# The first half of z with its last product on half the rows of the array, in an adaLN attention and gMLP block

## The chip, the cores and the metric

The kernel runs on one core of one Trainium2 chip. The core's engines work side by side, each through its own list in order: TensorE (PE: matmuls; PEld, the loads of their weights), VectorE (DVE), ScalarE (ACT), GpSimd (POOL), and SyncE (SP), which here issues the DMAs. An instruction that waits holds up everything behind it in its engine's list. The metric is the device time of one execution in microseconds (us); lower is better.

## The reference

```python
h = layernorm(x) * (1 + ca) + sa            # x: 2048 x 448
x = x + ga * attention(h)                   # 16 heads of 28
h = layernorm(x) * (1 + cb) + sb
z = gelu(h @ w_in)                          # w_in: 448 x 1792
z1, z2 = z[:, :896], layernorm(z[:, 896:])
g = w_sp @ z2 + b_sp[:, None]               # w_sp: 2048 x 2048
x = x + gb * ((z1 * g) @ w_out)             # w_out: 896 x 448
```

The six modulation vectors sa to gb come from `silu(c) @ w_mod`. The change lies in `z1`, and in one place at the start of `w_sp @ z2`.

## The kernel before

All is float32, and accuracy is kept by splitting each matmul operand into a high part (rounded by a copy to fp32r, the type of the matmul operands) and a low part (what is left, a subtraction on VectorE), and adding three products: high by high, high by low, low by high. For the 448 rows of `h` and `w_in` this makes 11 matmuls (`STEPS`, line 29): nine for the three full chunks of 128 rows, and two for the last 64 rows. For those, operand 6 of the features holds the high part in rows 0 to 63 and the low part in rows 64 to 127, operand 6 of the weights holds the high part twice, so step (6,6) gives high by high and low by high in one. Step (6,7) gives high by low: operand 7 of the weights has the low part in rows 0 to 63 and zeros in rows 64 to 127, so half of the array's rows do nothing.

The stages in order: modulation, layer norm and q, k, v; attention, head by head; the output projection `wo` (`wo_mm`, line 828) with layer norm two; the first half of z (`z1_unit`, line 1197); the second half (`z2_mm`, `z2_halves`, lines 1431 to 1451); the mix `w_sp @ z2` (line 1533), which goes through sums of blocks, so that fewer products are needed; gate and output.

**The first half of z.** The features are in four row groups g of 512 rows, `h2T[g]`, and z1 has seven column blocks f of 128, so there are 28 units, unit n = 7 g + f, in the order of n. A unit is 11 matmuls of 128x512 into one PSUM bank, a gelu on ScalarE (line 1204) into one of four slots of a buffer (slot n % 4), and a store of that slot to DRAM. Seven banks go round. Beside the units runs a list written out by hand, `H2_AT` (line 1239): after unit n it places the steps that make the features of later row groups. For group g they are: statistics and norm (`h2_stats`, `h2_norm`, VectorE with a power on POOL), a transpose on VectorE (`h2_turn`), a store to DRAM (`h2_put`, four DMAs), a load back in the shape that is wanted (`h2_load`, five DMAs), and `h2_group` (line 1184) for each chunk c: two activations (the scaled features, then their high part) and a subtraction on VectorE (the low part). Group 1 has its load after unit 0, its chunks 0 and 2 after unit 3, 1 after unit 4, 3 after unit 5. Group 2 has statistics to store after units 0 to 3, the load after 5, its chunks 0, 2, 1, 3 after units 8 to 11. Group 3: statistics to store after 4 to 7, load after 9, chunks after 13 to 16. Where steps of two groups stand behind one unit, the earlier group's come first. Between them stand the loads of `w_in`'s second half and its parts, and seven times (units 10 to 25) the load, the parts (`wout_part`, line 1227) and the store of `w_out`.

**The second half of z** has 16 tiles of 128 rows in two halves. It computes in pairs: `z2_halves` gives the (6,7) products of two halves to the upper and the lower 64 rows of the array. For that, `twin` holds the high part of the last 64 features a second time, in rows 64 to 127; DMAs write it (`twin_load`, line 1426) at the stage's start, from `h2T`. A tile's gelu is followed by its statistics, and by its norm `z2_norm` (line 1467), for tile 14 and 15 in the last rounds of the loop.

**The mix** begins with `w_split` (line 1409): ScalarE copies the high part of a block of w_sp, VectorE subtracts the low part.

Of the kernel before, what the change touches and what calls it, by code (L numbers as in the profile page):

```python
# [8 lines left out]
F32 = mybir.dt.float32  # L9
F32R = mybir.dt.float32r  # L10
AF = mybir.ActivationFunctionType
# [88 lines left out]
def tile_adaln_mha_gmlp(ctx, tc, x, wqkv, wo, w_in, w_spT, b_sp, w_out, cT, w_mod0, w_mod, out):  # L100
# [34 lines left out]
    def hview(heap, off, a, b):  # L135
        return heap[:, off : off + a * b].rearrange("p (a b) -> p a b", b=b)
# [13 lines left out]
    def sub(eng, dst, a, hi):  # L150
        eng.tensor_tensor(out=dst, in0=a, in1=hi.bitcast(F32), op=ALU.subtract)  # L151
# [872 lines left out]
    heapA = fh.tile([128, 8 * 896], F32R, name="heapA")  # L1024
    heapB = fh.tile([128, 8 * 896], F32R, name="heapB")
    xl3 = fh.tile([128, 7, 512], F32, name="xl3", tag="heapC")
    w1 = hview(heapA, 0, 8, 896)
    h2T = [hview(heapB, g * 3584, 7, 512) for g in range(2)]

# [114 lines left out]

    w1_lo(0, pool)
    w1_lo(1, pool)
# [37 lines left out]
    def h2_group(g, cs):  # L1184
        for c in cs:
            f, hi = t3b.tile([128, 512], F32, name="hfull"), h2T[g][:, c if c < 3 else 6, :]
            src = h2T[g][:, 3 + c, :].bitcast(F32)
            act.activation(f, src, AF.Identity, scale=cols["cb"][:, c : c + 1], bias=cols["sb"][:, c : c + 1])
            act.activation(hi, f, AF.Copy)
# [7 lines left out]
    def z1_unit(g, f):  # L1197
        ps_t = bank("z1_ps")
        for j, (a, b) in enumerate(STEPS):
            pe.matmul(ps_t, w1[:, b, f * 128 : (f + 1) * 128], h2T[g][:, a, :], start=j == 0, stop=j == NST - 1)  # L1200
# [3 lines left out]
        act.activation(zt, ps_t, AF.Gelu_apprx_tanh)  # L1204
        sp.dma_start(z1_scr[f * 128 : (f + 1) * 128, g * 512 : (g + 1) * 512], zt)

    for t in range(8, 12):
        wo_tile(t)
# [18 lines left out]
    def wout_part(f):  # L1227
        raw = wouts[f][0]
        dve.tensor_tensor(out=raw, in0=raw, in1=bcs["gb"], op=ALU.mult)
        hi, lo = (wo3.tile([128, D], F32R, name=f"wout_{i}") for i in range(2))  # L1230
        act.activation(hi, raw, AF.Copy)
        sub(dve, lo, raw, hi)
        wouts[f] = hi, lo
# [4 lines left out]

    H2_AT = {}
    for g, at_g in (  # L1240
        (1, ((0, h2_load), (3, h2_group, (0, 2)), (4, h2_group, (1,)), (5, h2_group, (3,)))),
        (2, ((0, h2_stats), (1, h2_norm), (2, h2_turn), (3, h2_put), (5, h2_load))),
        (2, ((8, h2_group, (0,)), (9, h2_group, (2,)), (10, h2_group, (1,)), (11, h2_group, (3,)))),
        (3, ((4, h2_stats), (5, h2_norm), (6, h2_turn), (7, h2_put), (9, h2_load))),
        (3, ((13, h2_group, (0,)), (14, h2_group, (2,)), (15, h2_group, (1,)), (16, h2_group, (3,)))),
    ):
        for n, fn, *a in at_g:
            H2_AT.setdefault(n, []).append((fn, g, *a))
    for g in range(NG):
        for f in range(7):  # L1250
            z1_unit(g, f)
            for fn, *a in H2_AT.get(7 * g + f, ()):
                fn(*a)
            if (g, f) in ((0, 4), (0, 5)):
                win_load(f - 4, (t3, t3b)[f - 4])
            for fn, n in ((wout_load, 10), (wout_part, 12), (wout_store, 13)):
                if 0 <= 7 * g + f - n < 14 and (7 * g + f - n) % 2 == 0:
                    fn((7 * g + f - n) // 2)
            if g == 1 and f in (3, 5):
                win_prep(f // 4, dve)  # L1260
                win_load(2 + f // 4, (t3, t3b)[f // 4])
            if g == 2 and f in (3, 5):
                win_prep(2 + f // 4, dve)
# [48 lines left out]
    def wouts_load(g):  # L1312
        for at_g, i, f in WOUT_AT:
            if at_g == g:
                if (i, f) == (0, 0):
                    tbuf.append(wp.tile([128, 5120], F32R, name="wouts", tag="tw", bufs=1))
                if (i, f) == (1, 4):
                    tbuf.append(wp.tile([128, 1536], F32R, name="wouts2", tag="once", bufs=1))
# [15 lines left out]
    def z_sum(p):  # L1334
        if p >= NM:
            return
        for d, a, b, op in MIX[p][0]:
            if d == ONCE:
                once[:] = [wp.tile([128, 1536], F32, name="once", tag="once", bufs=1).rearrange("p (t c) -> p t c", c=384)]
# [81 lines left out]
    tz = ph4.enter_context(tc.tile_pool(name="tz", bufs=2))  # L1421
    z_mv, z_st = {}, {}

    twin = wp.tile([128, 3, 512], F32R, name="twin", tag="once", bufs=1)

    def twin_load(g):
        sp.dma_start(twin[64:128, g % 3, :].bitcast(F32), h2T[g][0:64, 6, :].bitcast(F32))

    z2_ps = {}

    def z2_mm(t, hf, steps, start, stop):
# [42 lines left out]
    banks.append(7)  # L1474
    banks.sort(key=lambda k: k > 2)
    for g in range(3):
        twin_load(g)
    for t in range(NT + 1):
        if t < NT:
            for hf in range(2):  # L1480
                z2_mm(t, hf, STEPS[:-1], t % 4 < 2, t % 4 > 1)
                if t % 4 > 1:
                    z2_act(t, hf)
            if t % 4 > 1:
                z2_stats(t)
        if t % 4 == 1 and t < NT:
            for k in range(4):
                z2_halves(t - 1 + k, k > 1)
            if t == 1:
                twin_load(3)  # L1490
            for k in range(2):
                for hf in range(2):
                    z2_act(t - 1 + k, hf)
                z2_stats(t - 1 + k)
                z2_norm(t - 1 + k)
        if t % 4 == 3 or t % 4 == 0 and t:
            z2_norm(t - 1)
        if t == 8:
            heapB2.append(fh.tile([128, 8 * 896], F32R, name="heapB2", tag="heapB"))
            tbuf.append(wp.tile([128, 5120], F32, name="tbuf", tag="tw", bufs=1))  # L1500
        if t == 9:
            z_sum(0)
        if t in (10, 12):
            z_hi(t // 2 - 5)
            z_lo(t // 2 - 5)
        if t in (11, 13, 14):
            z6_split((11, 13, 14).index(t))
        if 9 <= t < 13:
            b_load(bts(t - 9), t - 9)
        if 11 <= t < 15:  # L1510
            w_load(t - 11)
        if t in (13, 15):
            w_split((t - 13) // 2)
# [209 lines left out]
```

## Time and profile before

| | |
|---|---|
| median of 3 runs | 1366.68 us (1366.61 to 1367.72) |
| the profiled execution | 1368.8 us, of which 1367.0 us are the span of the trace |
| PE / PEld busy | 1360.5 / 967.4 us |
| VectorE / ScalarE / GpSimd busy | 1111.7 / 803.5 / 357.7 us |
| granted TensorE clock | 0.999 on average |
| first half of z (L1200) | 308 matmuls, 898.78 to 968.9 us of the span |
| second half of z (L1437, L1451) | to 1038.6 us, then the mix |

A line such as L1200 is that line of the kernel. In a timeline each row has the start, the duration, the engine, the line, the operation with out<-in, how many were merged, and in brackets how long the engine stood idle before it and what ended that. SPq is SyncE's list of DMAs: a row there is the issue, and the data land later.

### The profile page before, as it was taken

How to read it: one execution, taken by the hardware profiler on the slowest of the kernel's cores; microseconds unless marked ns; L12 is line 12 of the kernel's file. 1: busy time of each engine (PE TensorE's matmuls, PEld its weight loads, DVE VectorE, ACT ScalarE, POOL GpSimd, SP SyncE). 2: the span in 40 equal slices, each digit the busy share in tenths (PEclk: the TensorE clock that was granted, in tenths of full speed). 3: DMA queues.
4: the chain of work that ended last, by engine and by line, in shares of the span. 5: the costliest groups of instructions: out<-in, count | busy, mean ns of one | idle time of the engine just before them, and what ended most of it. 6: DMA issues, size and time to landing. Idle time of an engine off the chain costs nothing.

```text
span 1367.0 us, 20774 instructions
## 1 busy us (share of the span) xinstructions
PE 1360.5 (100%) x7050; PEld 967.4 (71%) x7050; DVE 1111.7 (81%) x1764; ACT 803.5 (59%) x1475; POOL 357.7 (26%) x370
## 2 busy tenths in 40 slices
PE   9999999999999999999999999999999999999998
PEld 8888655555556555655565555788888888888898
DVE  7888999999999999999999991673458778999752
ACT  6624666776677667766776679556325545555411
POOL 2134434244544355654641002210011000000000
PEclk9999999999999999999999999999999999999999
DMA  7465747776677668777874110578714665788553
GB/s 281 142 169 182 222 132 225 210 233 198 217 228 224 189 203 250 231 214 222 247 219 118 43 44 24 182 215 269 246 31 155 223 200 176 258 289 260 177 165 109
DMA packets 144598, 260.72 MB, mean 191 GB/s; under 512 B 22184, under 2 KB 43050, under 8 KB 141946
## 3 DMA queue, kind: packets, MB, share of 16 engines
q1 hardware_dynamic: 141774, 255.22, 60.3%
q10 hardware_dynamic: 2718, 4.19, 0.9%
q8 instruction: 55, 0.90, 0.3%
q14 instruction: 51, 0.42, 0.1%
HBM read 177.67 MB, written 76.34 MB: 186 GB/s over the span
## 4 chain that ended last, share of the span: by engine, by line
PE 97%; DVE 2%; DMA 0%; issue 0%; ACT 0%; POOL 0%; POOLq 0%; SPq 0%; DVEq 0%; ACTq 0%
PE st_ps L745 19%; PE mt L713 17%; PE o_ps L760 17%; PE pq L408 5%; PE z_ps L1200 5%; PE acc L1540 5%; PE acc L1541 5%; PE acc L1539 5%; PE z_ps L1437 3%; PE wo_ps L832 3%; PE pv L390 2%; PE y_ps L1612 2%; PE y_ps L1610 2%; PE y_ps L1611 2%; PE acc L1549 1%; PE acc L1547 1%
## 5 line engine op out<-in xcount | busy, mean ns | idle before, releaser
L718 DVE TENSOR_REDUCE pm<-mt 128x1 f32<-128x512 f32 x1024 | 626.1, 677 | 7.8 <-PE mt L713 7.8
L749 ACT ACTIVATE P<-st_ps 128x512 f32<-128x512 f32 x1024 | 512.1, 648 | 201.4 <-PE st_ps L745 197.7
L745 PE MATMUL st_ps<-qst,kst 128*128 128x512 f32 x1024 | 408.4, 408 | 0.0
L713 PE MATMUL mt<-kst,qst 128*128 128x512 f32 x1024 | 401.5, 392 | 0.0
L745 PEld LDWEIGHTS st_ps<-qst,kst 128*128 128x128 f32 x1024 | 191.3, 188 | 127.9 <-DVE pm L718 53.2
L760 PE MATMUL o_ps<-P,V 128*32 128x512 f32 x2048 | 240.0, 597 | 0.0
L713 PEld LDWEIGHTS mt<-kst,qst 128*128 128x128 f32 x1024 | 192.4, 188 | 35.6 <-ACT P L749 1.5
L870 POOL TENSOR_TENSOR ws_raw<-ws_raw 128x512 f32<-128x512 f32 x112 | 144.0, 1290 | 176.0 <-DMA ws_raw<-in_w_spT_dram 108.3
L1414 ACT ACTIVATE heapB<-raw_sp 128x512 fp32r<-128x512 f32 x156 | 97.1, 630 | 99.4 <-PE acc L1541 75.9
L760 PEld LDWEIGHTS o_ps<-P,V 128*32 128x32 f32 x2048 | 58.9, 109 | 127.3 <-issue 91.3
L1539 PE MATMUL acc<-heapB,heapA 128*128 128x512 f32 x312 | 121.4, 389 | 0.0
L1541 PE MATMUL acc<-heapB,heapA 128*128 128x512 f32 x312 | 121.4, 389 | 0.0
L766 DVE TENSOR_TENSOR osb<-osb,o_ps 128x512 f32<-128x512 f32 x82 | 56.4, 687 | 61.9 <-PE o_ps L760 60.1
L151 DVE TENSOR_TENSOR heapB<-raw_sp,heapB 128x512 fp32r<-128x512 f32 x112 | 74.7, 687 | 27.9 <-ACT heapB L1414 27.7
L1540 PE MATMUL acc<-heapB,heapA 128*128 128x512 f32 x222 | 86.5, 390 | 0.5 <-DVE heapB L151 0.5
L1539 PEld LDWEIGHTS acc<-heapB,heapA 128*128 128x128 f32 x312 | 58.6, 188 | 12.1
L1541 PEld LDWEIGHTS acc<-heapB,heapA 128*128 128x128 f32 x312 | 58.6, 188 | 12.1
L408 PE MATMUL pq<-heapD,heapD 128*128 128x512 f32 x196 | 61.8, 390 | 0.0
L151 POOL TENSOR_TENSOR ws_raw<-ws_raw 128x512 fp32r<-128x512 f32 x44 | 56.6, 1287 | 3.5
L1540 PEld LDWEIGHTS acc<-heapB,heapA 128*128 128x128 f32 x222 | 41.7, 188 | 9.6 <-DVE heapB L151 0.9
L786 POOL TENSOR_TENSOR osb<-osb,rb 128x512 f32<-128x512 f32 x15 | 19.3, 1284 | 109.6 <-DMA rb<-r_scr 97.4
L408 PEld LDWEIGHTS pq<-heapD,heapD 128*128 128x128 f32 x196 | 36.7, 188 | 7.4
(229 smaller groups left out, 1637.7 us busy)
## 6 DMA issues: line engine op xcount, KB each, us to landing
ws_raw<-in_w_spT_dram SPq DMA_DIRECT2D x136, 256.0 KB
ws_scr<-ws_raw SPq DMA_DIRECT2D x112, 256.0 KB
ws_raw<-ws_scr SPq DMA_DIRECT2D x88, 256.0 KB
raw_sp<-ws_scr SPq DMA_DIRECT2D x88, 256.0 KB
raw_sp<-in_w_spT_dram SPq DMA_DIRECT2D x68, 256.0 KB
wl_scr<-ws_raw SPq DMA_DIRECT2D x44, 256.0 KB
kst<-qk_scr SPq DMA_DIRECT2D x45, 224.0 KB
qst<-qk_scr SPq DMA_DIRECT2D x45, 224.0 KB
```

The lines of the kernel that those rows point to most:

```text
L151: eng.tensor_tensor(out=dst, in0=a, in1=hi.bitcast(F32), op=ALU.subtract)
L408: pe.matmul(pq, wqk[:, b, m * 128 : (m + 1) * 128], hT[g][:, a, :], start=j == 0, stop=j == NST - 1)
L713: pe.matmul(mt, qst[h % 3][:, t * 128 : (t + 1) * 128], kst[h % 3][:, kb * 512 : (kb + 1) * 512], start=True, stop=True)
L718: dve.tensor_reduce(out=pms[h][:, t, kb : kb + 1], in_=mt, axis=AX.X, op=ALU.max)
L745: pe.matmul(st, kst[h % 3][:, kt * 128 : (kt + 1) * 128], qst[h % 3][:, qb * 512 : (qb + 1) * 512], start=True, stop=True)
L749: act.activation(p, st, AF.Exp, scale=SCALE)
L760: pe.matmul(o[32 * qb : 32 * qb + 32, :], V[:, u % NT, h, :], ptiles.pop((u, qb)), start=u == a, stop=u == e - 1)
L870: pool.tensor_tensor(out=a, in0=a, in1=b, op=ALU.add if W_SUMS[v][2] > 0 else ALU.subtract)
L1414: act.activation(hi, raw[0], AF.Copy)
L1539: pe.matmul(o, zh[:, c], hi, start=p < 2 and kt == 0, stop=False, skip_group_check=p > 1)
L1540: pe.matmul(o, zh[:, c], lo, start=False, stop=False, skip_group_check=p > 1)
L1541: pe.matmul(o, zl[:, c], hi, start=False, stop=kt == 3, skip_group_check=p > 1)
```

## The change

The first half of z is computed in pairs too. Units 0 to 3 of a row group run ten steps without the last and leave their banks open. Then three pairs of 64-row products follow: (0,1) and (2,3) close these four, (4,5) opens the next two. Units 4 and 5 run ten steps and close. Unit 6 keeps all eleven. An eighth bank makes room. The gelus and the stores of units 0 to 3 are all issued after the steps of `H2_AT` that stand behind unit 3. Those of units 4 to 6 stay behind their own unit, ahead of its steps. For group 0 `twin` is written by a DMA at the stage's start, ahead of the load for group 1. For groups 1 to 3 ScalarE writes it, in a third activation of `h2_group` for chunk 3; the slot is g % 3, so group 0's copy is loaded again ahead of the second half. Operand 7 of the weights has the low part in both halves of its rows, and the zeros go. Group 1's chunks move one unit up (behind 2, 3, 4). The parts of `w_out` get one buffer for two. The norms of tiles 14 and 15 move from the end of the second half into the mix, behind `w_split` of its blocks 2 and 3.

```diff
+    twin = ... tw.tile([128, 3, 512], F32R, name="twin", tag="once")
...
-    pool.memset(w1[64:128, 7, :].bitcast(F32), 0.0)
...
-            sub(eng, w1[0:64, 7, :], wraw[0][0:64, 3, :], w1[0:64, 6, :])
+            sub(eng, w1[:, 7, :], wraw[0][:, 3, :], w1[:, 6, :])
...
             act.activation(hi, f, AF.Copy)
+            if c == 3:
+                act.activation(twin[64:128, g % 3, :], f[64:128], AF.Copy)
...
+    def z1_halves(g, fs, start):
+        for f, src, r in zip(fs, (h2T[g][:, 6, :], twin[:, g % 3, :]), (slice(0, 64), slice(64, 128))):
+            if start:
+                z1_ps[f] = bank("z1_ps")
+            pe.matmul(z1_ps[f], w1[r, 7, f * 128 : (f + 1) * 128], src[r, :], start=start, stop=not start)
...
+    def z1_unit(g, f):
+        if (g, f) == (0, 0):
+            twin_load(0)
+        z1_mm(g, f, STEPS if f == 6 else STEPS[:-1], f < 4 or f == 6, f > 3)
+        if f == 3:
+            for fs in ((0, 1), (2, 3), (4, 5)):
+                z1_halves(g, fs, fs[0] == 4)
+
+    def z1_acts(g, f):
+        for k in range(4) if f == 3 else (f,) if f > 3 else ():
+            z1_act(g, k)
...
+    banks.append(7)
...
-        hi, lo = (wo3.tile([128, D], F32R, name=f"wout_{i}") for i in range(2))
+        hi, lo = (wo3.tile([128, D], F32R, name=f"wout_{i}", bufs=1) for i in range(2))
...
-        (1, ((0, h2_load), (3, h2_group, (0, 2)), (4, h2_group, (1,)), (5, h2_group, (3,)))),
+        (1, ((0, h2_load), (2, h2_group, (0, 2)), (3, h2_group, (1,)), (4, h2_group, (3,)))),
...
             z1_unit(g, f)
+            if f > 3:
+                z1_acts(g, f)
             for fn, *a in H2_AT.get(7 * g + f, ()):
                 fn(*a)
+            if f == 3:
+                z1_acts(g, f)
...
-    for g in range(3):
-        twin_load(g)
+    twin_load(0)
...
-        if t % 4 == 3 or t % 4 == 0 and t:
+        if t < NT - 1 and (t % 4 == 3 or t % 4 == 0 and t):
             z2_norm(t - 1)
...
         w_split(g + 2)
+        if g < 2:
+            z2_norm(NT - 2 + g)
```

`z1_act(g, f)` is the gelu into slot (7 g + f) % 4 and the store, as before.

More of the change, by code (lines that the diff above doesn't have):

```diff
@@ L1026, in tile_adaln_mha_gmlp, with twin_load @@
     xl3 = fh.tile([128, 7, 512], F32, name="xl3", tag="heapC")
+    tw = ctx.enter_context(tc.tile_pool(name="tw", bufs=1))
+    twin = tw.tile([128, 3, 512], F32R, name="twin", tag="once")
+    def twin_load(g):
+        sp.dma_start(twin[64:128, g % 3, :].bitcast(F32), h2T[g][0:64, 6, :].bitcast(F32))
     w1 = hview(heapA, 0, 8, 896)
@@ L1195, in tile_adaln_mha_gmlp, with z1_mm, z1_act @@
     zbuf = []
[L1197 to L1200, printed above, removed]
+    z1_ps = {}
+    def z1_mm(g, f, steps, start, stop):
+        if start:
+            z1_ps[f] = bank("z1_ps")
+        for j, (a, b) in enumerate(steps):
+            pe.matmul(
+                z1_ps[f],
+                w1[:, b, f * 128 : (f + 1) * 128],
+                h2T[g][:, a, :],
+                start=start and j == 0,
+                stop=stop and j == len(steps) - 1,
+            )
+    def z1_halves(g, fs, start):
+        for f, src, r in zip(fs, (h2T[g][:, 6, :], twin[:, g % 3, :]), (slice(0, 64), slice(64, 128))):
+            if start:
+                z1_ps[f] = bank("z1_ps")
+            pe.matmul(z1_ps[f], w1[r, 7, f * 128 : (f + 1) * 128], src[r, :], start=start, stop=not start)
+    def z1_act(g, f):
         if not zbuf:
@@ L1317, in wouts_load @@
                 if (i, f) == (1, 4):
-                    tbuf.append(wp.tile([128, 1536], F32R, name="wouts2", tag="once", bufs=1))
+                    tbuf.append(tw.tile([128, 1536], F32R, name="wouts2", tag="once"))
                 sp.dma_start((wouts_l if i else wouts_h)(f).bitcast(F32), wo2_scr[i, f])
@@ L1338, in z_sum @@
             if d == ONCE:
-                once[:] = [wp.tile([128, 1536], F32, name="once", tag="once", bufs=1).rearrange("p (t c) -> p t c", c=384)]
+                once[:] = [tw.tile([128, 1536], F32, name="once", tag="once").rearrange("p (t c) -> p t c", c=384)]
             dve.tensor_tensor(out=z_reg(d), in0=z_reg(a), in1=z_reg(b), op=ALU.add if op > 0 else ALU.subtract)
@@ L1422, in tile_adaln_mha_gmlp @@
     z_mv, z_st = {}, {}
-    twin = wp.tile([128, 3, 512], F32R, name="twin", tag="once", bufs=1)
-    def twin_load(g):
-        sp.dma_start(twin[64:128, g % 3, :].bitcast(F32), h2T[g][0:64, 6, :].bitcast(F32))
     z2_ps = {}
@@ L1472, in b_load @@
         sp.dma_start(dst, b_sp[tb * 512 : (tb + 1) * 512].rearrange("(o n) -> o n", o=1).broadcast_to([128, 512]))
-    banks.append(7)
     banks.sort(key=lambda k: k > 2)
-    for g in range(3):
-        twin_load(g)
+    twin_load(0)
     for t in range(NT + 1):
```

2 lines of the change are left out of this document (1 added, 1 removed).

## Prediction

> **What bounds the kernel now.** I read the page first, then the chain that ended last, then the timelines of each engine through the first half of z, the second half, and the start of the mix. The chain says which engine sets the end:
>
> ```profile
> PE 97%; DVE 2%; DMA 0%; issue 0%; ACT 0%; POOL 0%; POOLq 0%; SPq 0%; DVEq 0%; ACTq 0%
> ...
> 898.94 69.93 PE z_ps L1200 x308
> 968.88 8.11 PE z_ps L1437 x40
> ```
>
> TensorE has no room anywhere; in the changed stage it goes from one matmul to the next for 69.93 us, 69.93 / 308 = 0.227 us each. A 448-column product of the second half takes 8.11 / 40 = 0.203 us. So time falls only where TensorE gets less to do or waits less, and any new wait of TensorE costs its full length. The question is whether the features and the copies still arrive in time. That they only just do shows in one row of the weight loads, where row group 1 needs the low part of its chunk 3:
>
> ```profile
> 918.25 1.92 PEld L1200 LDWEIGHTS z_ps<-heapB,heapA 128*128 128x128 f32 x9 [0.23 <-DVE heapB L151]
> ```
>
> TensorE waited 0.2 us: this handover has no slack.
>
> **Part 1, the pairs.** Each row group loses three products (seven 64-row ones become three pairs and one full). What a pair costs is seen in the second half, where pairs run already:
>
> ```profile
> 976.62 0.37 PE L1437 MATMUL z_ps<-heapF,heapB 128*128 128x448 f32 x1
> 976.92 0.47 PE L1451 MATMUL z_ps<-heapF,heapB 64*128 64x448 f32 x1
> 976.92 0.47 PE L1451 MATMUL z_ps<-heapF,twin 64*128 64x448 f32 x1
> ...
> 977.92 0.48 PE L1437 MATMUL z_ps<-heapD,heapB 128*128 128x448 f32 x1
> ```
>
> The two of a pair start together, so the saving is real. From the last full product to the next full one, over four pairs, are 1.30 us; five slots of 0.203 would be 1.02, so a block of pairs costs 0.29 extra for entering and leaving. Here a block has three pairs: 3 x 0.227 - 0.29 = 0.39 us gained per row group, four times 1.6 us. A row group then takes 74 x 0.227 + 0.29 = 17.1 us.
>
> **Part 2, the late norms.** At the start of the mix TensorE waits for the low part of W's block 2, which stands on VectorE behind the two norms:
>
> ```profile
> 1042.55 0.39 PE L1539 MATMUL acc<-heapB,heapA 128*128 128x512 f32 x1
> 1043.43 0.50 PE L1540 MATMUL acc<-heapB,heapA 128*128 128x512 f32 x1 [0.50 <-DVE heapB L151]
> 1043.77 0.39 PE L1541 MATMUL acc<-heapB,heapA 128*128 128x512 f32 x1
> ...
> 1040.79 0.15 DVE L171 TENSOR_SCALAR rsz<-mvz 128x1 f32<-128x1 f32 x1
> 1040.86 0.74 DVE L1469 TENSOR_SCALAR z<-z,mvz,rsz 128x896 f32<-128x896 f32 x1
> 1042.03 0.74 DVE L1469 TENSOR_SCALAR z<-z,mvz,rsz 128x896 f32<-128x896 f32 x1 [0.44 <-POOL rsz L172]
> 1042.69 1.89 DVE L151 TENSOR_TENSOR heapB<-raw_sp,heapB 128x512 fp32r<-128x512 f32 x3
> ```
>
> From 1042.55 to 1043.77 are 1.22 us for two products of 0.227: 0.77 lost. With the norms behind it, the subtraction (a third of 1.89) runs from 1040.9 to 1041.6, a microsecond before it is needed. The norms then lie beside the products and are through when they were before, since VectorE does the same work in another order. Gain 0.8 us.
>
> **Part 3, the handover to row group 1.** Here the order of the lists matters more than the work. Four gelus now come at once into the four slots, and unit 4's gelu needs slot 0 again, so it waits until unit 0's store has landed. Behind it on ScalarE stands chunk 3 of group 1. Unit 0's store stands on SP behind the four DMAs of group 2 (`h2_put`), these wait for the transpose on VectorE, and the transpose now stands behind the low parts of chunks 0 and 2, which moved one unit up. Rows for the length of this chain, SP first, then ScalarE, then VectorE:
>
> ```profile
> 897.90 3.01 SPq L1091 DMA_DIRECT2D hs_scr<-turn  x4
> 901.01 2.68 SPq L1048 DMA_DIRECT2D x_scr<-xl  x2
> ...
> 904.86 1.27 SPq L1103 DMA_DIRECT2D heapB<-hs_scr  x3
> ...
> 922.20 0.85 SPq L1205 DMA_DIRECT2D z_scr<-z1t  x2
> 923.14 4.51 SPq L1091 DMA_DIRECT2D hs_scr<-turn  x4
> ...
> 931.42 1.27 SPq L1103 DMA_DIRECT2D heap<-hs_scr  x3
> ...
> 933.87 0.58 SPq L1205 DMA_DIRECT2D z_scr<-z1t  x1
> ...
> 963.08 0.60 SPq L1225 DMA_DIRECT2D raw_out<-in_w_out_dram  x1
> 964.75 0.94 SPq L1237 DMA_DIRECT2D wo_scr<-wout  x2
> ```
>
> ```profile
> 909.46 0.81 ACT L1188 ACTIVATE hfull<-heapB,col_sb,col_cb 128x512 f32<-128x512 f32 x1
> ...
> 911.67 0.63 ACT L1189 ACTIVATE heapB<-hfull 128x512 fp32r<-128x512 f32 x1
> ...
> 914.06 0.58 ACT L1204 ACTIVATE z1t<-z_ps 128x512 f32<-128x512 f32 x1
> ...
> 915.37 0.63 ACT L1189 ACTIVATE heapB<-hfull 128x512 fp32r<-128x512 f32 x1
> ...
> 927.51 0.60 ACT L1204 ACTIVATE z1t<-z_ps 128x512 f32<-128x512 f32 x1 [1.11 <-DMA z_scr<-z1t]
> ...
> 963.29 0.58 ACT L1231 ACTIVATE wout<-raw_out 128x448 fp32r<-128x448 f32 x1 [1.86 <-issue]
> ```
>
> ```profile
> 905.84 2.21 DVE L1087 STREAM_TRANSPOSE turn<-x 128x448 f32<-128x448 f32 x4
> ...
> 912.34 0.69 DVE L151 TENSOR_TENSOR heapB<-hfull,heapB 128x512 fp32r<-128x512 f32 x1 [0.68 <-ACT heapB L1189]
> ...
> 914.80 2.20 DVE L1056 BATCH_NORM_STATS2 st<-xl 128x6 f32<-128x448 f32 x4
> ...
> 920.80 2.21 DVE L1087 STREAM_TRANSPOSE turn<-xl 128x448 f32<-128x448 f32 x4
> ...
> 966.41 0.63 DVE L1229 TENSOR_TENSOR raw_out<-raw_out,bc_gb 128x448 f32<-128x448 f32 x1 [1.88 <-DMA raw_out<-in_w_out_dram]
> ```
>
> The row at 927.51 is the proof that a gelu waits for its slot's store: unit 10's waited for unit 6's, issued at 922.20, 5.3 us earlier. The shortest way of a DMA from issue to user here is 963.08 to 966.41, 3.3 us. These two are my bounds for a landing.
>
> Now the sum. The load for group 1 still issues at 904.86 (it waits for group 1's own store). Chunk 0 is there 3.3 us later at the earliest, 908.2, and at the latest at 909.46, where it was used without a wait; I take 908.5. Chunks 0 and 2 take 909.46 to 912.34 + 0.69, 3.6 us; the transpose 2.2 more: 914.3 instead of 908.1. The four DMAs take SP 3.0 us (897.90, with little else under way, as here): unit 0's store issues at 917.3, its gelu long done. Landing between 3.3 and 5.3, I take 4.3, since group 2's data are queued ahead of it: 921.6. Then unit 4's gelu, chunk 3's two activations (914.06 to 915.37 + 0.63) and the subtraction (0.69): 2.6 us, 924.2. TensorE wants that at 898.78 + 17.1 + 9 x 0.227 = 917.9. It waits 6.3 us, 6.1 more than before; bounds 4.8 and 8.1 with the ends above.
>
> Group 0's `twin` issues behind SP's two x stores, which end at 903.7, and lands at 907.0 to 909.0; its pairs come at 907.9. Up to 1.1 us could be lost there, but the end of the wait at 924.2 does not hang on it, so it costs nothing.
>
> **Part 4, the handover to row group 2.** The same again, and longer, because the chain starts late. Behind chunk 3's low part on VectorE stand group 3's statistics, norm and transpose: 914.80 to 920.80 + 2.21, 8.2 us. From the first DMA of that group's store to the load that waits for it 7.0 us (897.90 to 904.86) or 8.3 (923.14 to 931.42); the load's issues 2.45 (931.42 to 933.87). Only then SP comes to unit 7's store, 3.3 to 5.3 to land, then unit 11's gelu and chunk 3 of group 2, 2.6. Sum 23.6 to 26.9; I take 24.6, nearer the lower end, since little is queued ahead of the store. TensorE needs it one row group later, 17.1 us: it waits 7.5 us, bounds 6.5 and 9.8. Group 3's chunks stand ahead of the four gelus of group 2, so there is no third such wait; its price is 0, up to 1.
>
> **Part 5, what the waits leave behind.** After thin work TensorE's clock was seen to fall:
>
> ```profile
> 6.00:8.00 2.00, 1.38 (x13) 1.21 (x12) 1.86 (x7) 0.06 (x1) 0.71 (x1) 1.00 1.03 406
> 8.00:10.00 2.00, 2.00 (x16) 2.00 (x16) 1.79 (x6) 1.55 (x5) 0.90 (x1) 0.77 1.06 404
> 10.00:12.00 2.00, 2.00 (x11) 2.00 (x10) 1.93 (x8) 0.96 (x3) 0.00 (x0) 0.50 1.08 425
> 12.00:14.00 2.00, 2.00 (x15) 1.97 (x14) 0.64 (x3) 0.89 (x2) 0.00 (x0) 0.88 0.97 388
> ```
>
> The last number but two is the clock: 2 x (0.23 + 0.50 + 0.12) = 1.7 us of work lost. Each wait may bring that once. After the first it disappears in the second, whose end the other engines set; after the second it can count, 0 to 1.7. The parts of `w_out` with one buffer run late too: copy 0.58, subtraction about as long, the store's issue 0.94, its landing at least 3.3, so some 5.4 us for each of seven, 38 us from about 950, against a stage that ends near 981. The last gelus stand behind these copies and hold banks that the second half takes first. This is 0 to 4 us and overlaps with the slow clock; for both together I take 2.0, range 0 to 4.
>
> The Trainium skill ("TensorE: Matmul & The Clock Gate", section "Part 1: The HAM clock gate") says that an idle window of about 3.4 us halves the array's clock, and that about as long a busy one restores it. By that rule both waits, being longer, bring the slow clock for certain, and the second costs its 1.7 us; the sum without it would be some 1 us lower, since the late parts alone remain.
>
> **The sum.** -1.6 - 0.8 + 6.1 + 7.5 + 2.0 = +13.2. The profiled execution took 1368.8 us, 1.8 outside its span of 1367.0, and is 2.1 above the median: it would become 1382.0, the median 1366.68 + 13.2 = 1379.9. The ends: -2.4 + 4.8 + 6.5 = +8.9, 1375.6; -2.4 + 8.1 + 9.8 + 4 = +19.5, 1386.2.
>
> **Rivals.** *No new wait.* If unit 0's store lands by 917.9 - 2.6 = 915.3, chunk 3 is in time, and the old 0.2 goes too: -2.6, 1364.1. That decides it: a store whose issue the lists put at 917.3 would have to land 2 us earlier. For it speaks that before this buffer held ScalarE up once only, 1.1 us; against it the order on SP and the late transpose. 0.10.
>
> *The first wait alone.* If unit 11's gelu does not hold chunk 3 of group 2, the sum is -2.4 + 6.1 and the slow clock 1.7: +5.4, 1372.1. It needs the chain of part 4 in 17.1 us where the rows add up to 23.6. 0.13.
>
> *A third wait at the second half.* `twin` for its group 0 is loaded by SP behind all stores of z1 and of `w_out`. If these run 4 us late, its first pairs wait for that DMA, 3.3 to 5.3 us more: about +18, 1385. 0.12.
>
> The forecast keeps 0.65. That the pairs do not run together I leave out: the two rows at 976.92 exclude it.
>
> **Chances and range.** A difference of 0.2%, 2.7 us, is about what a measurement of this kernel can tell from none. The first rival's -2.6 lies just inside: 0.07 for no change, 0.03 for faster; the rest, 0.90, is slower. The range 1370 to 1387 takes in the second and third rival and both ends of the forecast, and leaves out the first.
>
> **What would show it.** Right: ScalarE's first gelu behind a burst idles for a DMA of z1's stores, near 917 and again near 940; TensorE's weight loads show a wait of about 6 us on the low part (the subtraction's line) in row group 1 and one of 7 to 8 in group 2; blocks of three pairs take about 1 us; in the mix the wait at the third block is gone. Wrong: if unit 4's gelu runs right behind the four without a wait, parts 3 and 4 fall; if the store lands but TensorE's wait is under 4 us, a landing is shorter than the rows say.

## The result and the profile after

The changed kernel takes 1379.59 us in the median (1378.88 to 1380.51), beside 1366.92 us for the kernel before on the same chip: a ratio of 1.0093, 95% interval [1.0082, 1.0104]. Of the kernel before these are five executions; a sixth took 5158.71 us, for a reason that the record does not show, and is left out. The change makes the kernel 12.7 us slower, where 13.2 were forecast. The profiled execution took 1378.88 us, of which 1377.1 are the span.

The chain that ended last no longer is TensorE alone. In its first line on the page, VectorE is as before, and DMAs, issue, SP's list and GpSimd, all at 0% before, are new:

```profile
PE 92%; DVE 2%; DMA 2%; issue 2%; SPq 1%; POOL 1%; ACT 0%; ACTq 0%; DVEq 0%; POOLq 0%
```

The timeline of TensorE's weight loads shows where it waited in the first half of z (start, duration, engine, line, operation, count; in brackets the idle time before and what ended it):

```profile
922.00 8.49 PEld L1210 LDWEIGHTS z_ps<-heapB,heapA 128*128 128x128 f32 x31 [6.09 <-DVE heapB L151]
...
945.26 8.53 PEld L1210 LDWEIGHTS z_ps<-heap,heapA 128*128 128x128 f32 x31 [4.59 <-DVE heap L151]
```

Two waits, both for the low part of chunk 3 (line 151 is the subtraction), one in row group 1 and one in row group 2; none in row group 3. TensorE's own rows give the first block of pairs, and the idle time ahead of the matmuls themselves (5.67 and 4.17 us, a little less than ahead of the loads):

```profile
906.08 0.49 PE L1222 MATMUL z_ps<-heapB,heapA 64*128 64x512 f32 x1
906.09 0.50 PE L1222 MATMUL z_ps<-twin,heapA 64*128 64x512 f32 x1
...
906.98 9.36 PE L1210 MATMUL z_ps<-heapB,heapA 128*128 128x512 f32 x40
...
922.00 8.91 PE L1210 MATMUL z_ps<-heapB,heapA 128*128 128x512 f32 x31 [5.67 <-DVE heapB L151]
...
945.26 5.08 PE L1210 MATMUL z_ps<-heap,heapA 128*128 128x512 f32 x14 [4.17 <-DVE heap L151]
```

The two products of a pair start together, and three pairs take 0.90 us (906.08 to 906.98). The windows of the same kernel (stretch, its length, busy time of PE, PEld, VectorE, ScalarE and GpSimd, then the granted clock, the DMA share and GB/s) show what each wait leaves behind:

```profile
915.00:920.00 5.00, 1.33 (x6) 0.75 (x5) 0.00 (x0) 0.74 (x2) 0.00 (x0) 0.86 0.93 285
920.00:925.00 5.00, 3.00 (x7) 2.42 (x8) 3.34 (x10) 2.90 (x5) 0.19 (x1) 0.50 0.80 251
925.00:930.00 5.00, 5.00 (x22) 4.10 (x22) 4.15 (x9) 2.79 (x4) 0.81 (x1) 0.96 0.83 240
940.00:945.00 5.00, 1.09 (x5) 0.56 (x3) 0.49 (x1) 2.42 (x4) 0.00 (x0) 1.00 0.98 299
945.00:950.00 5.00, 4.74 (x14) 3.77 (x15) 2.55 (x4) 3.61 (x7) 0.00 (x0) 0.66 0.63 228
```

When TensorE goes on at 922.00, its clock is at 0.50, for 3 us, and at 0.96 for the next 5: 3 x 0.50 + 5 x 0.04 = 1.7 us lost. After the second wait it is 5 x 0.34 = 1.7 again.

Stage by stage (first start of each stage's first line on TensorE, from its timeline):

| | before | after | difference |
|---|---|---|---|
| first half of z begins | 898.78 | 896.91 | -1.87 |
| first half lasts | 69.93 | 82.49 | +12.56 |
| second half lasts | 69.73 | 69.73 | 0 |
| mix to the end of the span | 328.56 | 327.97 | -0.59 |

The -1.87 is not the change's: the run with one buffer alone, below, has the code of before up to this stage and begins it at 896.38. Most of the 1.87 lies in the first 25 us of the kernel. The windows of before and of after for that stretch:

```profile
0.00:25.00 25.00, 22.82 (x126) 20.80 (x127) 17.27 (x53) 14.03 (x28) 6.34 (x13) 0.93 0.77 286
```

```profile
0.00:25.00 25.00, 23.63 (x132) 20.73 (x133) 18.46 (x57) 15.29 (x30) 7.14 (x13) 1.00 0.80 292
```

The profiled execution of before began at a clock of 0.93, which makes 25 x 0.07 = 1.75 of work lost at most; the product that follows (line 408) starts 1.33 later than after the change, at 24.55 against 23.22. The remaining 0.5 comes later, by the end of the output projection, and is not explained. The profiled executions of the late norms alone and of the last two runs below begin at 0.93 too. So the spans differ by only 10.1 us, while the medians differ by 12.7, and the stages by 12.56 - 0.59 = 12.0.

Now the links of the chain, in the order in which the prediction gave them. VectorE, ScalarE, SP (issue only), each from its timeline of the changed kernel:

```profile
908.61 0.69 DVE L151 TENSOR_TENSOR heapB<-hfull,heapB 128x512 fp32r<-128x512 f32 x1 [0.68 <-ACT heapB L1194]
909.22 2.22 DVE L1093 STREAM_TRANSPOSE turn<-x 128x448 f32<-128x448 f32 x4
...
921.25 0.69 DVE L151 TENSOR_TENSOR heapB<-hfull,heapB 64x512 fp32r<-64x512 f32 x1 [9.25 <-ACT heapB L1194]
921.98 2.21 DVE L1062 BATCH_NORM_STATS2 st<-xl 128x6 f32<-128x448 f32 x4
...
927.55 2.22 DVE L1093 STREAM_TRANSPOSE turn<-xl 128x448 f32<-128x448 f32 x4
...
944.51 0.69 DVE L151 TENSOR_TENSOR heap<-hfull,heap 64x512 fp32r<-64x512 f32 x1 [8.75 <-DMA raw_out<-in_w_out_dram]
```

```profile
905.73 0.82 ACT L1193 ACTIVATE hfull<-heapB,col_sb,col_cb 128x512 f32<-128x512 f32 x1 [10.85 <-DMA heapB<-hs_scr]
...
911.26 2.07 ACT L1228 ACTIVATE z1t<-z_ps 128x512 f32<-128x512 f32 x4
919.26 0.60 ACT L1228 ACTIVATE z1t<-z_ps 128x512 f32<-128x512 f32 x1 [5.93 <-DMA z_scr<-z1t]
919.76 0.80 ACT L1193 ACTIVATE hfull<-heapB,col_sb,col_cb 128x512 f32<-128x512 f32 x1
...
921.25 0.63 ACT L1196 ACTIVATE twin<-hfull 64x512 fp32r<-64x512 f32 x1
...
942.52 0.60 ACT L1228 ACTIVATE z1t<-z_ps 128x512 f32<-128x512 f32 x1 [7.88 <-DMA z_scr<-z1t]
943.02 0.80 ACT L1193 ACTIVATE hfull<-heap,col_sb,col_cb 128x512 f32<-128x512 f32 x1
```

```profile
911.46 3.01 SPq L1097 DMA_DIRECT2D hs_scr<-turn  x4
914.57 5.63 SPq L1229 DMA_DIRECT2D z_scr<-z1t  x5
...
929.79 3.01 SPq L1097 DMA_DIRECT2D hs_scr<-turn  x4
936.04 1.29 SPq L1109 DMA_DIRECT2D heap<-hs_scr  x3
937.38 1.09 SPq L1111 DMA_DIRECT2D heap<-hs_scr  x2
938.51 2.46 SPq L1229 DMA_DIRECT2D z_scr<-z1t  x4
```

Read them as one line. The transpose ends at 911.44, SP's four DMAs follow at 911.46, unit 0's store at 914.57; unit 4's gelu starts at 919.26, after 5.93 us in which ScalarE did nothing; chunk 3's first activation follows at 919.76, its subtraction ends at 921.94, and TensorE goes on at 922.00. The third activation, which writes `twin`, starts at 921.25 together with that subtraction, so it is no link of the chain. VectorE takes up group 3's statistics at 921.98, right behind that subtraction, and the same round begins again: transpose to 929.77, store, load, then unit 7's store at 938.51 and unit 11's gelu at 942.52. The 8.75 us that VectorE idled before 944.51 are put down to a load of `w_out`; by ScalarE's rows it is the gelu that came late.

The mix's third block, in the timelines of TensorE and VectorE: the subtraction now is ahead of the two norms, and the products follow each other at 0.23 us; the wait is gone.

```profile
1053.24 0.39 PE L1573 MATMUL acc<-heapB,heapA 128*128 128x512 f32 x1
1053.46 0.39 PE L1574 MATMUL acc<-heapB,heapA 128*128 128x512 f32 x1
1053.69 0.39 PE L1575 MATMUL acc<-heapB,heapA 128*128 128x512 f32 x1
```

```profile
1051.58 0.69 DVE L151 TENSOR_TENSOR heapB<-raw_sp,heapB 128x512 fp32r<-128x512 f32 x1
1052.19 0.74 DVE L1505 TENSOR_SCALAR z<-z,mvz,rsz 128x896 f32<-128x896 f32 x1
```

### The profile page after: what moved, and what is told of

Its sections match the earlier page's. It is cut to its first block, busy times and chain, and to the rows that moved or that the text cites. A ratio compares the mean times of both kernels' runs of the same rounds, so it can differ in the third digit from the quotient of the medians.

```text
span 1377.1 us, 20771 instructions
## 1 busy us (share of the span) xinstructions
PE 1361.9 (99%) x7050; PEld 965.7 (70%) x7050; DVE 1111.2 (81%) x1764; ACT 805.1 (58%) x1478; POOL 356.5 (26%) x369
## 4 chain that ended last, share of the span: by engine, by line
PE 92%; DVE 2%; DMA 2%; issue 2%; SPq 1%; POOL 1%; ACT 0%; ACTq 0%; DVEq 0%; POOLq 0%
PE st_ps L745 19%; PE mt L713 17%; PE o_ps L760 17%; PE acc L1574 5%; PE acc L1575 5%; PE acc L1573 5%; PE pq L408 5%; PE z_ps L1473 5%; PE z_ps L1210 2%; PE pv L390 2%; PE y_ps L1646 2%; PE y_ps L1645 2%; PE y_ps L1644 2%; PE acc L1582 1%; PE acc L1583 1%
```

## The experiments

The theory was the prediction's: the pairs and the late norms gain about 2.4 us, and the chain through VectorE's order, SP's order, the four slots and ScalarE's order makes chunk 3 late twice. The main rivals: that some other part (the single buffer of `w_out`, ScalarE's third activation, the pairs) costs the time, and that one link alone holds it. Each run was timed beside the kernel before.

| run | us | before | ratio, 95% interval | first half | second half |
|---|---|---|---|---|---|
| the change | 1379.59 | 1366.92 | 1.0093 [1.0082, 1.0104] | 82.49 | 69.73 |
| chunk 3 ahead of the gelus | 1374.77 | 1366.86 | 1.0058 [1.0044, 1.0072] | 80.90 | 69.73 |
| z1's stores first | 1376.01 | 1366.86 | 1.0068 [1.0054, 1.0082] | 79.34 | 69.73 |
| 14 slots | 1375.49 | 1366.86 | 1.0061 [1.0048, 1.0074] | 79.43 | 69.73 |
| chunks back | 1372.83 | 1366.86 | 1.0044 [1.0030, 1.0058] | 77.80 | 69.73 |
| late norms alone | 1366.28 | 1367.69 | 0.9994 [0.9985, 1.0003] | 69.91 | 69.73 |
| one buffer alone | 1367.69 | 1367.69 | 1.0003 [0.9994, 1.0012] | 69.93 | 70.09 |
| waits filled | 1377.02 | 1367.69 | 1.0073 [1.0059, 1.0086] | 81.62 | 69.72 |
| stores from ScalarE | 1373.77 | 1367.69 | 1.0049 [1.0036, 1.0063] | 76.24 | 71.34 |
| new orders | 1370.47 | 1367.01 | 1.0023 [1.0014, 1.0031] | 72.54 | 70.99 |
| orders and slots | 1368.39 | 1367.01 | 1.0007 [0.9998, 1.0016] | 70.73 | 70.99 |
| and two parts of w_out | 1366.12 | 1366.82 | 0.9991 [0.9982, 1.0000] | 69.35 | 69.72 |

The last two columns are each run's profiled execution (before: 69.93 and 69.73). It need not lie at the median: for the change it is the fastest of six, 0.7 us below the median, and with chunk 3 ahead of the gelus the slowest of five, 2.2 us above.

### Chunk 3 ahead of the gelus

```diff
-            if f > 3:
-                z1_acts(g, f)
             for fn, *a in H2_AT.get(7 * g + f, ()):
                 fn(*a)
-            if f == 3:
+            if f > 2:
                 z1_acts(g, f)
```

> The gelus of units 4 to 6 stand behind their unit's feature steps instead of ahead of them; nothing else differs from the changed kernel. Theory (unit 4's gelu, which waits for a slot's store, holds chunk 3 behind it on ScalarE): chunk 3 of group 1 follows the burst of gelus at once, its low part is there near 915.5, before 916.0 where TensorE wants it; both waits of 6.1 and 4.6 us and both slow clocks go, the gelus of units 4 and 11 still wait but hold up nobody; about 1364.7 us, 2.4 below the kernel before. Rival (the features themselves come late, because their loads or the transpose are late): the waits stay, 1378 or more.

The first wait is gone, as the theory said, so it was ScalarE's order that carried it to TensorE. But the time fell by only 4 to 5 us. TensorE's weight loads in this run:

```profile
936.91 8.44 PEld L1210 LDWEIGHTS z_ps<-heap,heapA 128*128 128x128 f32 x31 [3.95 <-DVE heap L151]
...
961.12 8.03 PEld L1210 LDWEIGHTS z_ps<-heap,heapA 128*128 128x128 f32 x30 [1.46 <-ACT z1t L1228]
```

The wait in group 2 is still there, 3.95 where the changed kernel has 4.59, and several in group 3 have come up, the longest of 2.43, the last of them for a bank. SP's list in the same run shows where the one in group 2 is from now: the five stores stand ahead of group 2's load, and the fifth can only be issued when its gelu has got its slot.

```profile
914.32 7.54 SPq L1229 DMA_DIRECT2D z_scr<-z1t  x5
...
922.43 1.33 SPq L1109 DMA_DIRECT2D heap<-hs_scr  x3
```

ScalarE then idles for that load until 927.76, and the next burst of gelus also stands ahead of group 2's chunk 3, whose first activation starts at 934.64. The expectation failed because it took out one link and forgot that the same slow slot also stands ahead of the next load.

### z1's stores first

```diff
             z1_unit(g, f)
-            if f > 3:
+            if f > 2:
                 z1_acts(g, f)
             for fn, *a in H2_AT.get(7 * g + f, ()):
                 fn(*a)
-            if f == 3:
-                z1_acts(g, f)
```

> The four gelus and their stores stand ahead of the feature steps of unit 3, so unit 0's store is ahead of group 2's four DMAs on SP. Theory: unit 0's store lands near 914.2, unit 4's gelu waits little, the first wait of TensorE falls from 6.1 to about 1 us. The second does not fall: unit 7's store still stands behind the load for group 3, which waits for that group's store; 6 to 7 us there with one slow clock. About 1373.7 us. Rival (only the four slots count, not SP's order): both waits stay, 1379. Rival (SP's order at group 2 is all): both go, 1365.

The first wait is gone again, by another link: here unit 0's store is ahead of group 2's DMAs. The second stays, and is longer. The weight loads:

```profile
941.72 8.67 PEld L1210 LDWEIGHTS z_ps<-heap,heapA 128*128 128x128 f32 x31 [8.63 <-DVE heap L151]
```

Undoing SP's order where it is undone, and the wait staying where SP still has the load for group 3 ahead of unit 7's store, is what the theory says; the time came 2.3 us higher than expected.

### Fourteen slots

```diff
-            zbuf.append(t3.tile([128, 4, 512], F32, name="z1t", tag="x3", bufs=3))
-        zt = zbuf[0][:, (7 * g + f) % 4, :]
+            zbuf.append(dpool.tile([128, 8 * 896], F32, name="z1t", tag="heapD1").rearrange("p (a b) -> p a b", b=512))
+        zt = zbuf[0][:, (7 * g + f) % 14, :]
```

> Fourteen slots for the gelus instead of four, in the memory that the attention output has left; orders as in the changed kernel. Theory: no gelu waits for a store, chunk 3 of groups 1 and 2 follows at once, both waits and both slow clocks go: about 1364.7 us, the first half of z in 68.4 us instead of 82.5. Rival (late features): waits of 4 us and more stay, 1375 or more.

No gelu waits for a store now, and the first wait is down to 0.30: the slots were a link. But TensorE waits 2.40 us in group 2, and 1.60, 0.43, 1.18 and, for a bank, 1.47 in group 3. Of its weight loads, the row behind the wait in group 2:

```profile
935.38 8.50 PEld L1210 LDWEIGHTS z_ps<-heap,heapA 128*128 128x128 f32 x31 [2.40 <-DVE heap L151]
```

The load for group 2 stands in SP's list behind the burst of stores, and ScalarE idles for it; later ScalarE idles for a load of `w_out` that SP issued late, with group 3's chunks behind it. Rows from ScalarE's timeline:

```profile
925.76 0.81 ACT L1193 ACTIVATE hfull<-heap,col_sb,col_cb 128x512 f32<-128x512 f32 x1 [8.86 <-DMA heap<-hs_scr]
...
944.53 0.58 ACT L1268 ACTIVATE wout<-raw_out 128x448 fp32r<-128x448 f32 x1 [8.64 <-DVE raw_out L1266]
```

So the expectation that slots alone would do was wrong.

### Group 1's chunks back to units 3, 4 and 5

```diff
-        (1, ((0, h2_load), (2, h2_group, (0, 2)), (3, h2_group, (1,)), (4, h2_group, (3,)))),
+        (1, ((0, h2_load), (3, h2_group, (0, 2)), (4, h2_group, (1,)), (5, h2_group, (3,)))),
```

> Group 1's chunks stand behind units 3, 4, 5 again, as in the kernel before; the rest is the changed kernel. Theory: the transpose for group 2 no longer stands behind chunk 0's and 2's low parts, group 2's four DMAs issue near 906 instead of 911.5, unit 0's store lands near 914 and the first wait is 2 to 3 us; group 3's statistics come before chunk 3's low part again, so the second is about 5. About 1373.7 us: the move one unit up made the change dearer, not cheaper. Rival (chunk 3 late by its own place in the list): a unit later means 2.3 us more wait, 1382.

With the transpose ahead of the low parts again, the waits are 0.35, 0.43 and 3.13 in group 1 and 3.86 in group 2, and the ratio falls from 1.0093 to 1.0044, 6.7 us. The line of the change that was to bring the chunks earlier made it dearer.

### The late norms alone, and one buffer alone

Both start from the kernel before. The first moves only the two norms:

```diff
-        if t % 4 == 3 or t % 4 == 0 and t:
+        if t < NT - 1 and (t % 4 == 3 or t % 4 == 0 and t):
...
         w_split(g + 2)
+        if g < 2:
+            z2_norm(NT - 2 + g)
```

> The kernel before with the norms of tiles 14 and 15 moved behind the splits of W's blocks 2 and 3, and nothing else. Theory: TensorE's wait at the third block of the mix (0.77 us lost) goes, 1366.4 us, 0.6 to 0.8 below the kernel before. Rival (the norms are wanted early, and their delay shows later in the mix): no gain or a loss.

The wait in the mix goes, and the mix to the end lasts 327.69 us (1365.7 - 1038.01) instead of 328.56. By its time alone the run is not told from no change: the interval holds 1. The second gives the parts of `w_out` one buffer:

```diff
-        hi, lo = (wo3.tile([128, D], F32R, name=f"wout_{i}") for i in range(2))
+        hi, lo = (wo3.tile([128, D], F32R, name=f"wout_{i}", bufs=1) for i in range(2))
```

> The kernel before with one buffer for two for the parts of w_out. Theory (units and features have enough slack beside it): no change, 1367.1 within 1 us. Rival (the copies on ScalarE wait for stores and push the features of group 3 past TensorE's need, or the last gelus past the second half's): 1 to 4 us slower.

Beside the old order of the units it costs nothing that the time shows (the second half of the profiled execution is 0.36 us longer).

### The waits filled with work

```diff
+            if (g, f, j) in ((1, 0, 9), (2, 0, 9)):
+                fill = bank("fill")
+                for _ in range((24, 26)[g - 1]):
+                    pe.matmul(fill, w1[:, 0, 0:128], h2T[0][:, 0, :], start=True, stop=True)
```

Products whose result nobody uses stand in the changed kernel ahead of the step that waits.

> The changed kernel, with 24 and 26 matmuls into a spare bank put ahead of the last step of units 7 and 14, where TensorE waits; they are not part of the result. Theory (TensorE's clock falls because it idles there): the clock stays full, the first wait with its filling ends at the same time, units 7 to 13 run 1.7 us faster and the second wait begins and is that much longer, and after it 1.7 us are gained: about 1377.9. Rival (the slow clock has another cause, or costs nothing): 1379.6 or more.

The chain is untouched (the loads that waited start at 921.79 and 945.89), TensorE stays busy until 0.55 and 1.12 us before, and the windows of this run show the clock that it keeps:

```profile
920.00:925.00 5.00, 4.87 (x22) 3.71 (x21) 3.34 (x10) 2.70 (x5) 0.40 (x1) 1.00 0.81 253
...
945.00:950.00 5.00, 4.30 (x19) 3.41 (x19) 3.20 (x5) 4.78 (x9) 0.00 (x0) 1.00 0.59 195
```

1.00 instead of 0.50 and 0.66: more work for TensorE, and yet less time, by (1.0093 - 1.0073) x 1367 = 2.7 us. That the slow clock comes from the idling is shown by the windows. The size is less sure in the time, since the two intervals overlap by a little. In the stage it is only 0.87 (82.49 to 81.62), with a second chain that took 24.1 us here (921.79 to 945.89) and 23.3 there; the profiled execution is the slowest of four here and the fastest of six there.

### Stores issued by ScalarE

```diff
-        sp.dma_start(z1_scr[f * 128 : (f + 1) * 128, g * 512 : (g + 1) * 512], zt)
+        (act if f < 4 else sp).dma_start(z1_scr[f * 128 : (f + 1) * 128, g * 512 : (g + 1) * 512], zt)
```

> The stores of units 0 to 3 of each group are issued by ScalarE right behind their gelus; SP does not have them. Four slots and the orders stay. Theory: unit 0's store no longer waits for group 2's DMAs, lands near 915, the first wait is 1 to 2 us; unit 7's store no longer waits for the load for group 3, the second wait is 0 to 2 us. Together about 1367 to 1368. Rival (the slots' number alone decides): both waits stay near 6 and 5 us, 1379.

The second wait falls from 4.59 to 0.27: SP's order was its cause, and the stores need no place in SP's list. The first falls only to 4.16. ScalarE's timeline shows why: each store's issue now stands between the gelus, and while the DMA engines are busy (94% from 913 to 917) one takes over a microsecond.

```profile
911.79 0.37 ACTq L1229 DMA_DIRECT2D z_scr<-z1t  x1
...
913.85 1.17 ACTq L1229 DMA_DIRECT2D z_scr<-z1t  x1
915.07 0.60 ACT L1228 ACTIVATE z1t<-z_ps 128x512 f32<-128x512 f32 x1 [1.25 <-issue]
915.70 1.12 ACTq L1229 DMA_DIRECT2D z_scr<-z1t  x1
916.92 0.60 ACT L1228 ACTIVATE z1t<-z_ps 128x512 f32<-128x512 f32 x1 [1.25 <-issue]
```

The first gelu starts at 911.16, unit 4's at 916.92, and chunk 3 behind it: ScalarE's own list has become the first wait. Behind that wait the clock stayed at 0.50 from 920 to 925, and the 31 loads that take 8.49 us in the changed kernel took 9.46. The second half, 1.6 us longer, waits for gelus that hold its banks. So the time is some 6 us above what was expected.

### New orders, then slots, then two parts

Three runs build on each other. The first changes only places in the lists: group 2's transpose and store one unit earlier, its load too; group 3's load two units later; `w_out`'s load one earlier.

```diff
-        (2, ((0, h2_stats), (1, h2_norm), (2, h2_turn), (3, h2_put), (5, h2_load))),
+        (2, ((0, h2_stats), (1, h2_norm), (1, h2_turn), (2, h2_put), (4, h2_load))),
...
-        (3, ((4, h2_stats), (5, h2_norm), (6, h2_turn), (7, h2_put), (9, h2_load))),
+        (3, ((4, h2_stats), (5, h2_norm), (6, h2_turn), (7, h2_put), (11, h2_load))),
...
-            for fn, n in ((wout_load, 10), (wout_part, 12), (wout_store, 13)):
+            for fn, n in ((wout_load, 9), (wout_part, 12), (wout_store, 13)):
```

> The changed kernel, four slots, with SP's and VectorE's lists in another order: group 2's transpose ahead of group 1's low parts and its store one unit earlier, its load behind unit 4 instead of 5, group 3's load behind unit 11 instead of 9 (so behind the stores of units 7 to 10), the loads of w_out one unit earlier. Theory (what stands ahead of a store or a load on SP sets when features come): unit 0's store issues near 912 and lands near 915.5, the first wait is 1 to 2 us and brings no slow clock, the second is gone, the load for group 2 lands early enough for its chunks; about 1366.5, within 1 us of the kernel before. Rival (four slots are too few under any order): waits of 4 us and more stay, 1372 or more.

With four slots and the same work the two waits are 0.97 and 1.58, from 6.09 and 4.59. So the orders on VectorE and SP carry most of the loss. The time is 4 us above what was expected: the second wait did not go altogether, and 1.64 and 1.27 us are now lost at the start of the second half, which waits for z1's last gelus. The next run adds the fourteen slots:

> The same orders, and fourteen slots for the gelus. With fourteen slots alone the first wait was gone, but group 2's load stood behind five stores and a load of w_in on SP, and w_out's first part held ScalarE until its own load landed; the orders take both away. Theory: no wait over 0.5 us is left in the first half of z, which takes 68.4 us; 1364.7 us, 2.4 below the kernel before: what the pairs and the late norms are worth by themselves. Rival (the pairs bring a wait that no order removes): 1367 or more.

The first half has no wait any more; the second still begins with one, of 2.11 us in the weight loads, and ScalarE's timeline shows what the last gelus stand behind:

```profile
968.51 0.51 PEld L1473 LDWEIGHTS z_ps<-heapD,heapB 128*128 128x128 f32 x3 [2.11 <-ACT z1t L1228]
```

```profile
962.35 0.58 ACT L1268 ACTIVATE wout<-raw_out 128x448 fp32r<-128x448 f32 x1 [2.67 <-DMA wo_scr<-wout]
966.91 0.58 ACT L1268 ACTIVATE wout<-raw_out 128x448 fp32r<-128x448 f32 x1 [3.98 <-DMA wo_scr<-wout]
967.39 2.04 ACT L1228 ACTIVATE z1t<-z_ps 128x512 f32<-128x512 f32 x4
```

Each copy of `w_out` waits until the part before it is stored, because there is one buffer. The time, 1368.39, lies where the rival put it, but the wait that is left is not the pairs'. The last run gives z1 ten slots and puts two buffers for the parts into the rest of that tile:

```diff
-        zt = zbuf[0][:, (7 * g + f) % 14, :]
+        zt = zbuf[0][:, (7 * g + f) % 10, :]
...
-        hi, lo = (wo3.tile([128, D], F32R, name=f"wout_{i}", bufs=1) for i in range(2))
+        o = 5120 + f % 2 * 1024
+        hi, lo = (z_buf()[:, o + 512 * i : o + 512 * i + D].bitcast(F32R) for i in range(2))
```

> The kernel with the new orders, but z1 has ten slots, and the parts of w_out have two buffers again, in what is left of that tile. Theory (the last waits of the run with fourteen slots come from w_out's one buffer: each of ScalarE's copies waits for the store of the part before it, 3.0, 2.7 and 4.0 us in its list, and the last gelus stand behind them): those three waits go, the second half's first products find their banks free, and the 2.1 + 0.2 us that TensorE waited there are gain: 1368.4 - 2.3 = 1366.1, a ratio of 0.999 to the kernel before. Rival (the gelus themselves are late, since four or three of them come in a burst and ScalarE has other copies between them): the copies' waits go, but TensorE still waits about 2 us for gelus, and the time stays at 1368.4, a ratio of 1.001. A second rival: ten slots are too few, and a gelu waits for its slot's store again, as it did with four; then a wait of 1 us or more is seen in row group 1 or 2.

The waits on the stores of `w_out` are gone, and the second half begins without one; 0.62 us remain in group 1. The median is 0.7 us below that of the kernel before, the ratio of 0.9991 makes 1.2 us, and the interval ends at 1.0000: this is the best that the change came to here, at the edge of what can be told from no change. Its weight loads also give the length of a row group of the changed kind without any wait, from unit 4 of one group to unit 4 of the next:

```profile
942.77 15.96 PEld L1215 LDWEIGHTS z_ps<-heap,heapA 128*128 128x128 f32 x71 [0.37 <-issue]
...
959.98 6.89 PEld L1215 LDWEIGHTS z_ps<-heap,heapA 128*128 128x128 f32 x31 [0.37 <-issue]
```

## Why the prediction was right, and where its terms were off

**Part 1, the pairs.** 17.21 us (959.98 - 942.77) instead of 69.93 / 4 = 17.48: 0.27 for each row group, 1.1 us in all, where 1.6 were said. The block's entry and exit cost 0.1 us more than in the second half.

**Part 2, the late norms.** 0.59 us from the mix to the end in the changed kernel, 0.87 alone; 0.8 said.

**Part 3, the handover to row group 1.** Right link by link, with ends that balance. The chain began 1.0 us early: chunk 0 was used 2.8 us after its load's issue (902.95 to 905.73), less than the 3.3 that the prediction took for the shortest way of a DMA, and the transpose ended at 911.44 where 914.3 - 1.87 = 912.4 was said. Unit 0's store to its gelu took 4.69 us (914.57 to 919.26) where 4.3 was taken; gelu to low part 2.68, said 2.6. The wait is 6.1 us, said 6.3. That this is the cause was shown by breaking the chain at three places, ScalarE's order, SP's order and the slots: each took the first wait away, to 0.3 us at most. The fourth, VectorE's order, was not broken alone: the new orders (6.09 to 0.97) move entries of SP's list with it, and the chunks put back (0.35, 0.43 and 3.13) move ScalarE's.

**Part 4, the handover to row group 2.** The mechanism was right, the size was not: 4.59 us, where 7.5 were taken and 6.5 was the lower bound. The chain took 23.3 us (921.94 to 945.20), a little below its lower end of 23.6, since the store and the load that waits for it went faster: 6.25 us (929.79 to 936.04) where the rows of before had 7.0 and 8.3. And TensorE needed the part at 945.26 - 4.59 = 940.67, which is 18.7 us after 922.00 and not 17.1, because it ran slowly after the first wait. Part 5 had said that the first slow clock disappears in the second wait; part 4's number had not been lowered for it. In the total the two belong together: 4.59 + 1.6 is 6.2 against 7.5.

**Part 5, what the waits leave behind.** The slow clock came with both waits and cost 1.7 us each time, as the four rows of before gave it. The Trainium skill ("TensorE: Matmul & The Clock Gate", section "Part 1: The HAM clock gate") has an idle window of about 3.4 us halve the clock; the changed kernel's trace agrees, with 0.50 behind 5.67 us of idling, and 0.66 in the mean of the 5 us behind 4.17. Another run does not: with fourteen slots the clock was 0.66 from 935 to 940 too, behind a wait of 2.40 us, which is shorter than that window. There the measurement decides. The late parts of `w_out` cost nothing, in the changed kernel (the second half lasts 69.73 in both) and, as far as the time shows, alone. The longer first half probably hid them; in the runs where the two waits were gone they did come up, with 2.1 us, and a second buffer took that away.

**The sum.** +13.2 was forecast. With the measured terms it is -1.1 - 0.6 + 6.1 + 4.6 + 3.4 = +12.4, the slow clock counted after both waits; the medians differ by 12.7. This takes the idle time ahead of the loads; with that ahead of the matmuls, 5.67 and 4.17, it is +11.5, so the sum closes to about 1 us. Misses balance: part 4 was 2.9 too long, part 5, with 2.0 for two causes, was 1.4 too short, and parts 1 and 2 gained 0.7 less than said. That the total came nearer than its terms is luck. The stage's pieces close in the same way: 4 x 17.21, the idle times 5.67 and 4.17, and 3.4 are 82.1, and it lasted 82.49.

**The rivals.** *No new wait* and *the first wait alone* fell with the two rows of the weight loads. *A third wait at the second half* did not come in the changed kernel. Group 0's `twin`, put at nothing, cost nothing: TensorE ran through its first pairs at 906.08. The pairs, the third activation and the one buffer are all still in the run with the new orders, which takes 9 us less than the change, so none of them holds the bulk of the loss; the buffer holds a part of what is left, the 2.1 us above.

The mended versions gain little because little is there to gain. The pairs and the norms add up to 1.7 us and 0.62 of a wait remain, so about 1.1 is due; 0.7 was measured by the medians and 1.2 by the ratio. What stays open is whether even that is a gain, since the interval reaches from 0 to 2.5 us.

## What to carry to other kernels

Before work is gathered into a burst (four gelus at once here), write down for each queue what then stands behind the burst, and what the burst stands behind: the price lies there and not in the instructions that are saved. A chain that runs through several lists is not mended at one link; the next late transfer shows at once, so look at all the lists before a gain is booked. Buffers that are given up because they cost nothing now may be the cover that the next improvement needs.

## What the runs showed of the hardware

In the changed kernel, waits of TensorE of 4 to 6 us brought some 3 us of work at half clock each, 1.7 us of work lost, and unneeded matmuls in their place kept the clock at 1.00. The length of a wait alone did not decide. A wait of 2.40 us (fourteen slots, group 2) brought the slow clock, 0.66 in the mean from 935 to 940; one of 3.13 us (chunks back, group 1) left it at 1.00 from 915 to 925; and behind one of 4.16 us (stores from ScalarE) it stayed at 0.50 from 920 to 925. No run here shows what does decide.

The issue of a DMA is not of one length. In the run with stores from ScalarE it was 0.34 to 0.37 us on ScalarE's list, and 1.12 to 1.17 two stores later, with the DMA engines 94% busy. On SP, the stores of units 0 to 4 in the changed kernel took 0.32 to 1.47 us each; the rest of the 5.63 us of their row is the wait of the fifth for its gelu.
